# Two groups of weight tiles by seven products, and prelu by a minimum on GpSimd, in blocks 3 to 5 of a retention and feed-forward kernel

## The chip, the cores and the metric

The kernel runs on one core of a Trainium2 chip. The metric is the device time of one execution in microseconds. An execution uses five engines: TensorE (PE in the profile, PEld for its weight loads), VectorE (DVE), ScalarE (ACT), GpSimd (POOL) and SyncE (SP), which only issues transfers. Each engine runs its own list of instructions in order, and semaphores make one wait for another.

## The reference

The first part is a linear attention with a decaying state; the second is a feed-forward layer with a prelu that has one alpha for each of its 2048 hidden columns.

```python
for t in range(S):                                   # 768 steps, 4 batches, 8 heads, 64 wide
    state = gamma * state + k[:, :, t] (x) v[:, :, t]
    y[:, :, t] = scale * q[:, :, t] @ state
x = y.transpose(0, 2, 1, 3).reshape(B * S, H * D)    # 3072 tokens by 512
h = x @ w_in                                         # 512 by 2048
g = np.maximum(h, 0.0) + alpha * np.minimum(h, 0.0)
out = g @ w_out                                      # 2048 by 512
```

## The kernel before

**Blocks.** The 3072 tokens are cut into six blocks (n = 0 to 5) of 512. The attention is done in chunks of 128 tokens, four a block; its result for block n + 1 is made while the feed-forward of block n runs, and lands transposed in `xT`, in two halves of 256 tokens. The order of all instructions is written out by hand: Python generators (`ffn1_mix`, `seven`) yield after each matmul, and `tick(gen, m)` draws m matmuls from one, so the order of the calls in the source is the order on every engine.

**First product, one tile.** A tile of the 2048 hidden columns has 128 of them, so there are sixteen. A whole tile is four matmuls of 512 tokens into one PSUM bank (`full`, L919), then a relu of the negative on ScalarE (L906) and `oma * relu(-h) + h` on VectorE, with oma = 1 - alpha (L910). That is the prelu.

**First product, seven products.** From block 3 on, tiles 0, 1, 8 and 9 are done by a Winograd-Strassen scheme: seven products of sums of halves of x and of w_in replace eight. One product is four matmuls of 256 columns (`part`, L934). The sums of w_in (`win_sum`, four of them) are made once, on GpSimd in block 2; the four sums of x (`x_sum`) for each block, two on VectorE and two on GpSimd. Three PSUM banks are used: products 1, 6, 7 and 4 add up in one (b), product 2 has one (a), products 5 and 3 add up in one (c). After products 1, 6 and 7 ScalarE copies bank b to SBUF (`kept`, L966), and the next product that adds to b must wait for that copy. Then VectorE adds another bank to a copy (L970): for product 2, for product 7 (it reads bank c, so product 3 must wait for it), and for product 3. The three results C get their prelu in `ends`: a relu on ScalarE, then on GpSimd a product with oma (L983) and a sum (L989). The fourth result, in bank b after product 4, is done on ScalarE and VectorE like a whole tile. `MIX` (L897) is the order: 1 to 7 are the products, 0 is a whole tile.

**Second product.** `seven` (L783) multiplies the prelu's result G (`gt`) with w_out by the same scheme, each product being 16 matmuls of 256 columns (L790). It needs sums of G (`g_sums`, L763, with the operation itself in L738): which 0 and 1 make `gs`, 2 makes `third`, 3 subtracts into `gt`; part 0 and 1 are the two halves of the tiles, None is both. The order on PE is: two products of plain G (L790 `ops<-wout,gt`), one of `gs` 1, one of `gs` 0, one of `third`, and two more of G; output sums (`os`, L820) lie between.

**Around it.** In blocks 2 to 4, PE does the scores and states of the next block's chunks between the first and the second product. The k and q of a chunk are scaled to f16 first (`scaled`: one GpSimd operation, L137, or eight on ScalarE, L129), and `turn` transposes them by DMA. In `ffn1_mix`, after eight matmuls, the last chunk (u0 + 3) is scaled, k and q both on GpSimd. `decay` and `sums` carry the state on VectorE (L203, L215) and GpSimd (L217).

Of the kernel before, what the change touches and what calls it, by code (L numbers as in the profile page):

```python
# [9 lines left out]
FP = mybir.dt.float32  # L10
# [5 lines left out]
SUB = mybir.AluOpType.subtract  # L16


@with_exitstack
def kernel(  # L20
# [10 lines left out]
    nc = tc.nc  # L31
# [49 lines left out]
    oma_sb, seen, warm = small[:, 0:NFT], small[:, 32:48], small[:, 64:65]  # L81
    w_in_all = sbp.tile([128, 4, d_ff], F16, tag="win", name="win")
# [785 lines left out]
    wins, xsum = [], []  # L868

    def win_sum(i, eng):  # L870
        if not wins:
            wins.append(sbp.tile([128, 4, 2, 256], F16, tag="gs2", bufs=1, name="wins"))
        t = wins[0]
        a = [[w_in_all[:, 2 * l : 2 * l + 2, 1024 * j : 1024 * j + 256] for l in range(2)] for j in range(2)]
# [22 lines left out]
    MIX = [1, 2, 0, 5, 6, 0, 7, 0, 0, 4, 3] + 8 * [0]  # L897

    def ffn1_mix(n):
        fts = [f for i in range(2, HF) for f in (i, i + HF)]  # L900
        x = xT[n]
        h, bk, later = {}, {}, []
# [31 lines left out]
        def part(s, i):  # L934
# [4 lines left out]
            b, w, t = bk[at], wins[0], xsum[0]  # L939
            for ff in range(2):  # L940
                f = slice(128 * ff, 128 * ff + 128)
                f8 = slice(1024 + 128 * ff, 1152 + 128 * ff)
                for kk in range(2):
                    lhsT, rhs = (
                        (w_in_all[:, kk, f], x[:, 0, kk, :]),
                        (w_in_all[:, 2 + kk, f], x[:, 0, 2 + kk, :]),
                        (w[:, 3, kk, f], x[:, 1, 2 + kk, :]),
                        (w_in_all[:, 2 + kk, f8], t[:, 3, kk, :]),
                        (w[:, 0, kk, f], t[:, 0, kk, :]),
                        (w[:, 1, kk, f], t[:, 1, kk, :]),  # L950
                        (w[:, 2, kk, f], t[:, 2, kk, :]),
                    )[i - 1]
                    nc.tensor.matmul(  # L953
                        out=b[:, 256 * ff : 256 * ff + 256],
                        lhsT=lhsT,
                        rhs=rhs,
                        start=first and ff == 0 and kk == 0,
                        stop=kk == 1,
                        skip_group_check=True,
                    )  # L960
                    yield
# [5 lines left out]
            if i in (2, 7, 3):  # L967

                to = h[{2: 1, 7: 7, 3: 6}[i]]
                nc.vector.tensor_tensor(out=to, in0=bk["a" if i == 2 else "c"], in1=to, op=ADD)  # L970
                later.append((s, to, {2: (0, 0), 7: (HF, 256), 3: (0, 256)}[i]))
            if i == 4:
                hm = relu(b, "hm")
                for ff in range(2):
                    at = slice(256 * ff, 256 * ff + 256)
                    prelu(HF + ff, slice(0, 256), hm[:, at], b[:, at])

        def ends():
            while later:
                _, to, (f, t) = later.pop(0)  # L980
                hm = relu(to, "uv")
                hv, v = [a.rearrange("p (f t) -> p f t", f=2) for a in (hm, to)]
# [6 lines left out]
                nc.gpsimd.tensor_tensor(  # L989
                    out=gt_at(n, slice(f, f + 2), slice(t, t + 256)), in0=hv, in1=v, op=ADD  # L990
                )

        for s, step in enumerate(MIX):
            yield from part(s, step) if step else full()
            if later and s - later[0][0] >= (2 if later[0][0] > 1 else 3):
                ends()
# [207 lines left out]
    ucast(3, 1, A)  # L1204
    w_sums(1, G, [0])
# [45 lines left out]
    for n in range(1, NBLK):  # L1251
        more = n + 1 < NBLK
        u0 = UB * (n + 1)
        if n == 2:
# [14 lines left out]
            for i in range(4):  # L1269
                win_sum(i, G)  # L1270
            for _ in gen:
                pass
        elif n > 2:
# [3 lines left out]
            if more:  # L1277

                scaled(u0 + 3, "k", G)
# [22 lines left out]
        if more:  # L1302
# [118 lines left out]
```

## Time and profile before

| what | us |
|---|---|
| median of 3 runs | 200.2 |
| the three runs | 198.96, 200.2, 201.06 |
| span of the profiled execution | 196.5 |

The page names no time of the profiled execution other than its span. A row of a timeline has the start and duration in us, the engine, the line of the kernel, the operation, output and inputs, and the shape; `x8` means eight of them run on, with the duration from the first start to the last end; in brackets stands the idle time before it. A row of the groups by line has the busy time, then the mean of one in ns. An operation's duration holds the time that it waits for its operands once it has been issued. PE rows overlap by the pipeline: what a stretch costs is the distance from its start to the next row's start. `hm` is a relu's result, `kept` a copy of a bank, `os` an output tile, `hps` and `ops` are PSUM banks.

### The profile page before, as it was taken

To read this page: it belongs to the slowest core of one execution; us is meant where nothing else is said; L and a number is where in the kernel's file an instruction comes from. 1 tells how busy PE (TensorE), PEld (TensorE's weight loads), DVE (VectorE), ACT (ScalarE), POOL (GpSimd) and SP (SyncE) were. 2 spreads that over 40 slices of the span, in tenths; PEclk is the share of its full clock that TensorE was granted. 3 is DMA by queue.
4 is the path that set the end of the run, shared out by engine and by line. 5 is a ranking of instruction groups with operands and counts; after the bars stand their busy time and mean duration, and the time that the engine had idled before them with its cause. 6 is when DMAs were issued, how large, how long until landed. Compare 5 with 4: busy or idle time off the path is not lost.

```text
span 196.5 us, 6453 instructions
## 1 busy us (share of the span) xinstructions
PE 188.7 (96%) x2668; PEld 131.3 (67%) x2668; DVE 151.4 (77%) x258; ACT 119.1 (61%) x265; POOL 149.0 (76%) x151
## 2 busy tenths in 40 slices
PE   7879999999999989999999999999999999999993
PEld 5657544558668878644788754888654888655882
DVE  2697987164989897588978879967789977798922
ACT  3377763238676954477549987749987334686210
POOL 3368989999999576999379999499999296678000
PEclk9999999999999999999999999999999999999999
DMA  6999999999898999999998999992860013100014
GB/s 170 326 361 400 408 384 284 328 360 195 180 244 132 184 306 225 212 282 240 226 222 201 213 224 224 244 215 83 184 189 2 3 57 110 57 0 0 0 58 160
DMA packets 92749, 38.78 MB, mean 197 GB/s; under 512 B 70176, under 2 KB 88624, under 8 KB 92720
## 3 DMA queue, kind: packets, MB, share of 16 engines
q1 hardware_dynamic: 91440, 37.36, 75.8%
q10 hardware_dynamic: 1280, 1.01, 1.6%
q8 instruction: 21, 0.34, 0.7%
q14 instruction: 8, 0.07, 0.1%
HBM read 27.35 MB, written 6.29 MB: 171 GB/s over the span
## 4 chain that ended last, share of the span: by engine, by line
PE 75%; DVE 5%; POOL 5%; DMA 4%; ACT 3%; issue 2%; SPq 2%; POOLq 1%; DVEq 0%; ACTq 0%
PE ops L790 25%; PE hps L620 12%; PE hps L923 11%; PE hps L648 9%; PE ops L715 5%; PE hps L953 3%; DMA qu<-in_q_dram 2%; SPq L340 2%; POOL gt L989 2%; ACT kq L129 2%; PE ops L684 2%; DMA kt<-kq 2%; POOL hm L983 2%; PE ya L522 1%; POOLq L1416 1%
## 5 line engine op out<-in xcount | busy, mean ns | idle before, releaser
L790 PEld LDWEIGHTS <-gt 128*128 128x128 f16 x320 | 30.6, 98 | 4.1
L923 PE MATMUL hps<-xT,win 128*128 128x512 f16 x144 | 33.0, 379 | 0.0
L910 DVE SCALAR_TENSOR_TENSOR gt<-hm,small,hps 128x512 f16<-128x512 f32 (+1 forms) x42 | 28.7, 706 | 5.1 <-ACT hm L906 3.8
L790 PE MATMUL ops<-wout,gt 128*128 128x256 f16 x240 | 28.4, 273 | 0.0
L906 ACT ACTIVATE hm<-hps 128x512 f32<-128x512 f32 x39 | 23.1, 593 | 6.1 <-PE hps L923 5.4
L620 PE MATMUL hps<-xT,win 128*128 128x512 f16 x112 | 24.5, 379 | 0.0
L630 DVE SCALAR_TENSOR_TENSOR gt<-hm,small,hps 128x512 f16<-128x512 f32 x28 | 20.9, 747 | 3.8 <-ACT hm L629 0.9
L923 PEld LDWEIGHTS <-win 128*128 128x128 f16 x144 | 14.1, 98 | 14.4
L137 POOL TENSOR_TENSOR kq<-kqs,tab 128x512 f16<-128x512 f32 x23 | 23.6, 1050 | 0.0
L629 ACT ACTIVATE hm<-hps 128x512 f32<-128x512 f32 x28 | 16.7, 597 | 9.3 <-PE hps L620 9.3
L662 DVE SCALAR_TENSOR_TENSOR gt<-hm,small,hps 128x256 f16<-128x256 f32 x40 | 17.1, 477 | 4.3 <-ACT hm L657 4.3
L808 ACT ACTIVATE kept<-ops 128x512 f32<-128x512 f32 x15 | 9.0, 597 | 18.4 <-PE ops L790 18.4
L620 PEld LDWEIGHTS <-win 128*128 128x128 f16 x112 | 11.0, 98 | 12.8
L217 POOL TENSOR_TENSOR t<-ss,tab 128x256 f16<-128x256 f32 x13 | 8.7, 670 | 14.0 <-DVE ss L215 14.0
L790 PE MATMUL ops<-wsum,gs 128*128 128x256 f16 x160 | 19.1, 273 | 0.2 <-DVE os L820 0.2
L738 POOL TENSOR_TENSOR gt<-gt,gs 128x1024 f16<-128x1024 f16 x8 | 17.0, 2125 | 2.3 <-PE ops L790 2.3
L648 PE MATMUL hps<-xT,win 128*128 128x256 f16 x160 | 18.3, 273 | 0.0
L129 ACT ACTIVATE kq<-kqs,tab 128x64 f16<-128x64 f32 x72 | 18.1, 337 | 0.0
L648 PEld LDWEIGHTS <-win 128*128 128x128 f16 x160 | 15.4, 98 | 2.4
L790 PEld LDWEIGHTS <-gs 128*128 128x128 f16 x160 | 15.1, 98 | 2.4 <-issue 0.4
L820 DVE TENSOR_TENSOR os<-ops,kept 128x512 f32<-128x512 f32 (+1 forms) x17 | 10.5, 624 | 6.5 <-ACT kept L808 4.6
L657 ACT ACTIVATE hm<-hps 128x512 f32<-128x512 f32 x20 | 11.8, 597 | 5.5 <-PE hps L648 3.9
(132 smaller groups left out, 388.5 us busy)
## 6 DMA issues: line engine op xcount, KB each, us to landing
out_dram<-os SPq DMA_DIRECT2D x20, 256.0 KB, 3.5
wi<-in_moe_w_in_dram SPq DMA_DIRECT2D x8, 512.0 KB, 7.7
wo<-in_moe_w_out_dram SPq DMA_DIRECT2D x8, 512.0 KB, 8.5
kqs<-in_k_dram SPq DMA_DIRECT2D x16, 256.0 KB, 4.3
kqs<-in_q_dram SPq DMA_DIRECT2D x16, 256.0 KB, 4.2
vs<-in_v_dram SPq DMA_DIRECT2D x16, 256.0 KB, 4.9
ku<-in_k_dram SPq DMA_DIRECT2D x4, 256.0 KB, 4.1
qu<-in_q_dram SPq DMA_DIRECT2D x4, 256.0 KB, 4.7
```

Source lines behind the costliest of these rows:

```text
L129: eng.activation(out=kqs[u][:, a, h % 4, h // 4, :], in_=staged[u][nm][:, h, :], func=COPY, bias=0.0, scale=tab[:, H * a + h : H * a + h + 1],
L137: eng.tensor_tensor(out=kqs[u][:, a].rearrange("p i r d -> p r i d"), in0=staged[u][nm].rearrange("p (r i) d -> p r i d", i=4), in1=tab[:, ...
L620: nc.tensor.matmul(out=hps, lhsT=w_in_all[:, hp, 128 * ft : 128 * ft + 128], rhs=xT[n][:, :, hp, :], start=(hp == 0), stop=(hp == 3),)
L629: nc.scalar.activation(out=hm, in_=hps, func=RELU, bias=0.0, scale=-1.0)
L630: nc.vector.scalar_tensor_tensor(out=gt_at(n, ft, slice(0, TB)), in0=hm, scalar=oma_sb[:, ft : ft + 1], in1=hps, op0=MULT, op1=ADD,)
L648: nc.tensor.matmul(out=hps[:, 256 * (ft - f0) : 256 * (ft - f0) + 256], lhsT=w_in_all[:, hp, 128 * ft : 128 * ft + 128], rhs=xT[n][:, half ...
L662: nc.vector.scalar_tensor_tensor(out=gt_at(n, f, to), in0=hm[:, at], scalar=oma_sb[:, f : f + 1], in1=hps[:, at], op0=MULT, op1=ADD,)
L738: eng.tensor_tensor(out=out, in0=a, in1=b, op=op)
L790: nc.tensor.matmul(out=bk[:, 256 * t : 256 * t + 256], lhsT=a[:, f, 128 * t : 128 * t + 128], rhs=w[:, f, :], start=first and f == 0 and ( ...
L906: nc.scalar.activation(out=t, in_=src, func=RELU, bias=0.0, scale=-1.0)
L910: nc.vector.scalar_tensor_tensor(out=gt_at(n, f, cols), in0=hm, scalar=oma_sb[:, f : f + 1], in1=src, op0=MULT, op1=ADD,)
L923: nc.tensor.matmul(out=hps, lhsT=w_in_all[:, hp, 128 * ft : 128 * ft + 128], rhs=x[:, :, hp, :], start=(hp == 0), stop=(hp == 3),)
```

## The change

In `ffn1_mix` a second group, tiles 2, 3, 10 and 11, is done by seven products as well, so eight whole tiles are left of twelve. `MIX` gets one list for each group; one whole tile, not two, stands between products 7 and 4. The relu and the GpSimd product of the ends are replaced by two GpSimd operations, (alpha - 1) * min(C, 0), one for each tile of 256 columns, and the sum after them stays. The ends are issued right behind their VectorE sum, no longer two or three steps later. `noma_sb` = alpha - 1 is made once on GpSimd.

Work is moved with it. All four sums of x go to VectorE. The four sums of w_in of the second group are made on VectorE in block 2. The scaling of k of chunk u0 + 3 goes from GpSimd to ScalarE. In blocks 3 to 5 the sums of G are four on VectorE (part 1, then part 0), and `third` part 0 is on GpSimd behind the ends; in block 5 part 1 of `third` is there too.

```diff
-    MIX = [1, 2, 0, 5, 6, 0, 7, 0, 0, 4, 3] + 8 * [0]
+    MIX = [1, 2, 0, 5, 6, 0, 7, 0, 4, 3], [1, 0, 2, 5, 6, 0, 7, 0, 4, 3]
...
-                hm = relu(to, "uv")
...
-                nc.gpsimd.tensor_tensor(
-                    out=hv,
-                    in0=hv,
-                    in1=oma_sb[:, f : f + 2].unsqueeze(2).to_broadcast([128, 2, 256]),
-                    op=MULT,
...
+        def end(to, f, t):
+            hm = sbp.tile([128, 512], FP, tag="uv", bufs=2, name="hm")
+            for ff in range(2):
+                at = slice(256 * ff, 256 * ff + 256)
+                nc.gpsimd.tensor_scalar(
+                    out=hm[:, at],
+                    in0=to[:, at],
+                    scalar1=0.0,
+                    scalar2=noma_sb[:, f + ff : f + ff + 1],
+                    op0=MIN,
+                    op1=MULT,
                 )
...
-            if s == 15:
-                g_sums(n, 0, 2 if n + 1 < NBLK else 0, nc.gpsimd)
-            if s == 17 and n + 1 == NBLK:
-                g_sums(n, 0, 1, nc.vector)
...
-                scaled(u0 + 3, "k", G)
+                scaled(u0 + 3, "k", A)
...
-            ((0, 1), (1, 0), (1, 1)) if n == 1 else ((None, 0), (None, 1)) if more else ((1, 0), (1, 1))
+            ((0, 1), (1, 0), (1, 1))
+            if n == 1
+            else ((None, 0), (None, 1))
+            if n == 2
+            else ((1, 0), (1, 1), (0, 0), (0, 1))
         ):
             g_sums(n, p, w, V)
+        if n > 2:
+            g_sums(n, 0, 2, G)
         if not more:
-            g_sums(n, 0, 2, V)
-            g_sums(n, 1, 2, V)
+            g_sums(n, 1, 2, G)
...
+                if n == 2:
+                    win_sum(1, 0, V)
+                    win_sum(1, 1, V)
                 tick(gen, 15)
                 decay(pb[1])
+                if n == 2:
+                    win_sum(1, 2, V)
+                    win_sum(1, 3, V)
...
-                x_sum(n + 1, 2, G)
-                x_sum(n + 1, 3, G)
+                x_sum(n + 1, 2)
+                x_sum(n + 1, 3)
```

ScalarE at the start of block 3 before, from the last xT copy on; `kq` is the scaled k and q, `kept<-hps` the copy of product 1, then of product 6:

```order
L600 ACTIVATE xT_2348<-yb 128x4x64
L129 ACTIVATE kq_2379<-kqs_2004,tab 128x64 x8
L966 ACTIVATE kept<-hps 128x512
L906 ACTIVATE hm<-hps 128x512
L966 ACTIVATE kept<-hps 128x512
L906 ACTIVATE hm<-kept 128x512
L906 ACTIVATE hm<-hps 128x512
L966 ACTIVATE kept<-hps 128x512
```

The same place now:

```order
L602 ACTIVATE xT_2349<-yb 128x4x64
L131 ACTIVATE kq_2380<-kqs_2005,tab 128x64 x8
L979 ACTIVATE kept<-hps 128x512
L131 ACTIVATE kq_2562<-kqs_2010,tab 128x64 x8
L918 ACTIVATE hm<-hps 128x512
L979 ACTIVATE kept<-hps 128x512
L918 ACTIVATE hm<-hps 128x512
L979 ACTIVATE kept<-hps 128x512
```

Eight more scalings stand between the first copy and the first relu, and the relu of `kept` is gone.

VectorE at the end of block 2 before; the first `os` frees the bank of PE's last product, `xT` is the input of block 3:

```order
L203 TENSOR_TENSOR t_15_2365<-t_15_2355,sta 128x256
L820 TENSOR_TENSOR os<-ops,kept 128x512
L215 TENSOR_TENSOR ss_2401<-t_15_2365,stb 128x256
L820 TENSOR_TENSOR os<-kept,ops 128x512
L599 TENSOR_TENSOR xT_2348<-ya,zs 128x4x64
```

And now:

```order
L205 TENSOR_TENSOR t_15_2366<-t_15_2356,sta 128x256
L740 TENSOR_TENSOR wins_2382<-win 128x512
L740 TENSOR_TENSOR wins_2382<-wins_2382,win 128x512
L822 TENSOR_TENSOR os<-ops,kept 128x512
L217 TENSOR_TENSOR ss_2405<-t_15_2366,stb 128x256
L740 TENSOR_TENSOR wins_2382<-win 128x512
L740 TENSOR_TENSOR wins_2382<-win,wins_2382 128x512
L822 TENSOR_TENSOR os<-kept,ops 128x512
L601 TENSOR_TENSOR xT_2349<-ya,zs 128x4x64
```

Two sums of w_in stand ahead of each output sum, and all four ahead of xT.

GpSimd in block 5 before, to the end of the program:

```order
L983 TENSOR_TENSOR hm<-hm,small 128x512
L989 TENSOR_TENSOR gt_3856<-hm,kept 128x2x256
L983 TENSOR_TENSOR hm<-hm,small 128x512
L989 TENSOR_TENSOR gt_3856<-hm,kept 128x2x256
L983 TENSOR_TENSOR hm<-hm,small 128x512
L989 TENSOR_TENSOR gt_3856<-hm,kept 128x2x256
L738 TENSOR_TENSOR gs_3965<-gt_3856 128x1024
```

The last three of six ends, and what follows them, now:

```order
L996 TENSOR_SCALAR hm<-kept,small 128x256 x2
L1004 TENSOR_TENSOR gt_3924<-hm,kept 128x2x256
L996 TENSOR_SCALAR hm<-kept,small 128x256 x2
L1004 TENSOR_TENSOR gt_3924<-hm,kept 128x2x256
L996 TENSOR_SCALAR hm<-kept,small 128x256 x2
L1004 TENSOR_TENSOR gt_3924<-hm,kept 128x2x256
L740 TENSOR_TENSOR third<-gt_3924 128x1024 x2
```

Three more ends stand ahead of these, and two halves of `third` come behind them in place of a half of `gs`.

More of the change, by code (lines that the diff above doesn't have):

```diff
@@ L81 @@
     oma_sb, seen, warm = small[:, 0:NFT], small[:, 32:48], small[:, 64:65]
+    noma_sb = small[:, 80:96]
     w_in_all = sbp.tile([128, 4, d_ff], F16, tag="win", name="win")
@@ L863, in seven, with win_sum @@
             late_stores.append(put(0, 1, c, u2))
[L868 to L874, printed above, removed]
+    wins, xsum = {}, []
+    def win_sum(g, i, eng):
+        if g not in wins:
+            tag = ("gs2", "wi1")[g]
+            wins[g] = sbp.tile([128, 4, 2, 256], F16, tag=tag, bufs=1, name=f"wins{g}")
+        t = wins[g]
+        a = [
+            [
+                w_in_all[:, 2 * l : 2 * l + 2, 1024 * j + 256 * g : 1024 * j + 256 * g + 256]
+                for l in range(2)
+            ]
+            for j in range(2)
+        ]
         x, y, op = (
@@ L894, in x_sum @@
         minus(eng, t[:, i], x, y)
-    MIX = [1, 2, 0, 5, 6, 0, 7, 0, 0, 4, 3] + 8 * [0]
+    MIX = [1, 2, 0, 5, 6, 0, 7, 0, 4, 3], [1, 0, 2, 5, 6, 0, 7, 0, 4, 3]
     def ffn1_mix(n):
-        fts = [f for i in range(2, HF) for f in (i, i + HF)]
+        mix = [i and (g, i) for g, m in enumerate(MIX) for i in m]
+        groups = len(MIX)
+        fts = [f for i in range(2 * groups, HF) for f in (i, i + HF)]
+        mix += [0] * (len(fts) - mix.count(0))
         x = xT[n]
-        h, bk, later = {}, {}, []
+        h, bk = {}, {}
         def relu(src, tag):
@@ L1204 @@
     ucast(3, 1, A)
+    nc.gpsimd.tensor_scalar(
+        out=noma_sb, in0=oma_sb, scalar1=-1.0, scalar2=0.0, op0=MULT, op1=ADD
+    )
     w_sums(1, G, [0])
```

44 lines of the change are left out of this document (22 added, 22 removed).

## The prediction

> **What bounds the kernel.** I read the page's busy table first, then the timeline of each engine in blocks 2 to 5, then the groups by line for prices.
>
> ```profile
> span 196.5 us, 6453 instructions
> PE 188.7 (96%) x2668; PEld 131.3 (67%) x2668; DVE 151.4 (77%) x258; ACT 119.1 (61%) x265; POOL 149.0 (76%) x151
> ```
>
> PE is busy 96% of the span, so a wait of PE of any length is paid almost in full, and a matmul saved is gained in full. The other engines have room on average only; what matters is which of them ends last where PE needs it. PE in block 5, from product 7 of the seven on (start, duration, then the instruction):
>
> ```profile
> 170.89 1.89 PE L923 MATMUL hps<-xT,win 128*128 128x512 f16 x8
> 172.61 0.60 PE L953 MATMUL hps<-xsum,win 128*128 128x256 f16 x4
> 173.05 0.60 PE L953 MATMUL hps<-xT,wins 128*128 128x256 f16 x4
> 173.49 7.07 PE L923 MATMUL hps<-xT,win 128*128 128x512 f16 x32
> 180.39 3.67 PE L790 MATMUL ops<-wout,gt 128*128 128x256 f16 x32
> 183.91 1.91 PE L790 MATMUL ops<-wsum,gs 128*128 128x256 f16 x16
> ```
>
> From start to next start: 32 matmuls of 512 columns take 6.90 us, 0.216 each, a whole tile (four) 0.86; four of 256 columns take 0.44, 0.11 each.
>
> **The saving.** A second group replaces 16 x 0.216 = 3.45 us by 28 x 0.11 = 3.08: 0.37 us a block, 1.1 us over three blocks.
>
> **Product 3 waits (all three blocks).** Product 3 writes into the bank that the sum for product 7 reads, and that sum needs the copy of product 7. ScalarE and VectorE there, in block 5:
>
> ```profile
> 170.28 0.62 ACT L906 ACTIVATE hm<-kept 128x512 f32<-128x512 f32 x1
> 170.80 0.59 ACT L906 ACTIVATE hm<-hps 128x512 f32<-128x512 f32 x1
> 171.28 0.60 ACT L966 ACTIVATE kept<-hps 128x512 f32<-128x512 f32 x1
> ...
> 171.42 0.75 DVE L910 SCALAR_TENSOR_TENSOR gt<-hm,small,hps 128x512 f16<-128x512 f32 x1 [1.12 <-ACT hm L906]
> 172.09 0.68 DVE L970 TENSOR_TENSOR kept<-hps,kept 128x512 f32<-128x512 f32 x1
> ```
>
> Before, product 7 ended at 170.89, the sum at 172.77, and product 3 came at 173.05 behind two whole tiles and product 4: no wait. Now one whole tile stands there, so PE is at product 3 0.86 us sooner, at 172.2. The relu of C (170.28) is gone from ScalarE, so the copy ends near 171.7, but the sum still stands behind the prelu of the tile before (ends near 171.95) and ends near 172.6. PE waits 0.45 us, in each of the two groups: 0.9, against 0.37 saved. Block 5's first product then takes 0.55 us longer to its end, at 181.0.
>
> **Product 7 waits (blocks 3 and 4).** Eight scalings of k stand newly on ScalarE between the copy of product 1 and the first relu. Block 3 before:
>
> ```profile
> 109.33 2.01 ACT L129 ACTIVATE kq<-kqs,tab 128x64 f16<-128x64 f32 x8
> 111.23 0.58 ACT L966 ACTIVATE kept<-hps 128x512 f32<-128x512 f32 x1
> 111.71 0.58 ACT L906 ACTIVATE hm<-hps 128x512 f32<-128x512 f32 x1
> 112.50 0.60 ACT L966 ACTIVATE kept<-hps 128x512 f32<-128x512 f32 x1 [0.20 <-PE hps L953]
> ...
> 113.16 0.60 PE L953 MATMUL hps<-xsum,wins 128*128 128x256 f16 x4
> ...
> 123.84 3.67 PE L790 MATMUL ops<-wout,gt 128*128 128x256 f16 x32
> 127.34 3.22 PE L790 MATMUL ops<-wsum,gs 128*128 128x256 f16 x28
> ```
>
> The new eight run 111.73 to 113.63 (1.90 to the next start, as 109.33 to 111.23), the relu 0.49, the copy of product 6 114.1 to 114.7. Product 7 adds to the bank that is copied: it starts at 114.75 and not at 113.16, 1.6 us late. Behind it come product 3's waits, 0.3 and 0.5 (in the first group VectorE is freer), less the 0.37: the stage ends 2.0 us later, so 123.84 becomes 125.8. Taking this off GpSimd saves it 1.05 us, which hides nothing here, since GpSimd then waits for that late sum. The data of k is loaded long before; the transpose behind it on SP, and the loads behind that, serve the next block.
>
> **GpSimd's chain.** An end of C was a relu on ScalarE and two GpSimd operations; now it is two TENSOR_SCALAR of 128x256 and the add. No row shows that operation. Rows near it, and what follows on VectorE:
>
> ```profile
> L1070 POOL CAST win<-wi 128x256 f16<-128x256 f32 x5 | 2.0, 436 | 0.0
> L989 POOL TENSOR_TENSOR gt<-hm,kept 128x512 f16<-128x512 f32 x9 | 11.5, 1273 | 0.7
> ...
> 0.80 0.36 POOL L1075 MEMSET mi<- 128x320 f16 x1 [0.29 <-POOLq L1405]
> ...
> 128.21 0.61 POOL L217 TENSOR_TENSOR t<-ss,tab 128x256 f16<-128x256 f32 x1 [3.37 <-DVE ss L215]
> ...
> 122.70 2.13 POOL L738 TENSOR_TENSOR third<-gt 128x1024 f16<-128x1024 f16 x1
> ...
> 181.97 0.74 DVE L910 SCALAR_TENSOR_TENSOR gt<-hm,small,hps 128x512 f16<-128x512 f32 x1
> 182.74 0.69 DVE L738 TENSOR_TENSOR gs<-gt 128x1024 f16<-128x1024 f16 x1
> ```
>
> I take 0.41 from the CAST (one source, same size; 2.0 us for five); the ends are the memset's 0.36 and the two-source 0.61. An end costs 2 x 0.41 + 1.27 = 2.09 us. The Trainium skill, GPSIMD Engine Reference, section Elementwise, gives a one-source loop 1.03 cycles an element, an estimate of 0.22 us here; by it the sum below would be 17.5 and not 18.9. In block 5 the sum for product 7 is there at 172.6, and five ends follow almost without a gap: 172.65 + 5 x 2.09 = 183.1. In block 3 it is there at 116.8 and they end at 127.5 (127.25, and a gap of 0.25 ahead of the sum for product 3). Block 4 has the same order and is taken like block 3. Only then can the last two of VectorE's four sums of G run, and the first product of G sums (183.91 and 127.34 above) waits for the last of them.
>
> **The four sums against GpSimd.** They read two SBUF tensors, as the sums of x do:
>
> ```profile
> 135.59 3.04 POOL L137 TENSOR_TENSOR kq<-kqs,tab 128x512 f16<-128x512 f32 x3
> ...
> 137.79 1.13 DVE L738 TENSOR_TENSOR xsum<-xT 128x512 f16<-128x512 f16 x1
> ...
> 166.44 0.43 DVE L738 TENSOR_TENSOR xsum<-xT 128x512 f16<-128x512 f16 x1
> ```
>
> Alone the sum takes 0.43; beside GpSimd it takes 1.13 and ends at 138.92, 0.29 after GpSimd's operation (135.59 + 3.04). So such a sum waits out the GpSimd operation it meets, and each sum that waits for the one before lets one GpSimd operation in. Block 5: the last prelu ends at 182.6, sum 1 waits for the end's add and is done at 183.7, third 0 runs to 185.7 (2.13), sum 2 to 186.2, third 1 to 188.15, sum 3 to 188.7, sum 4 to 189.4. PE starts at 189.45 and not at 183.91: 5.5 us, with the 0.55 in it. Blocks 3 and 4: sum 1 ends at 128.0, third 0 at 130.0 (the other third comes later there), then 130.5, 131.1, 131.85; PE starts at 131.9 and not at 127.34: 4.6 us each, the 2.0 in it. Behind the four sums on VectorE stand the state sums, an output sum and the masks of the next pair; PE asks for the masks 28 matmuls after that start (3.22 us), and both move alike, so nothing is added; third 1 and the two subtractions behind it on GpSimd move with the state sums by the same 4.6.
>
> Two pages of the Trainium skill differ here. Perfetto Trace Analysis, section Optimizing Scalar/DVE Operations, gives the lock to a 2-port VectorE operation, which a TENSOR_TENSOR is not: by it the sums would not wait, and the time would be the second rival's, 207.1. SBUF — State Buffer, section Who interferes with whom, adds operations with two SBUF inputs, and with it the time is 219.1; the trace's 1.13 against 0.43 is on that side.
>
> **Four sums of w_in on VectorE in block 2.** The same waiting:
>
> ```profile
> 105.27 2.13 POOL L738 TENSOR_TENSOR gt<-gt,gs 128x1024 f16<-128x1024 f16 x1
> 107.35 3.23 POOL L137 TENSOR_TENSOR kq<-kqs,tab 128x512 f16<-128x512 f32 x3
> ...
> 105.35 0.42 DVE L203 TENSOR_TENSOR t<-t,sta 128x256 f16<-128x256 f16 x1 [0.18 <-POOL t L217]
> 106.09 0.69 DVE L820 TENSOR_TENSOR os<-ops,kept 128x512 f32<-128x512 f32 x1 [0.31 <-ACT kept L808]
> ...
> 108.26 0.42 DVE L599 TENSOR_TENSOR xT<-ya,zs 128x256 f16<-128x256 f32 x1 [0.36 <-ACT zs L591]
> ...
> 107.00 0.38 PE L790 MATMUL ops<-wout,gt 128*128 128x256 f16 x2
> ```
>
> Sum 1 stands behind the row at 105.35, waits until 107.4 and ends at 107.7; one scaling goes in (1.08), sum 2 ends at 108.9. The output sum of 106.09 comes at 108.9, and PE's last product, which writes into the bank it reads, at 109.6 and not 107.00: 2.6 us. Sums 3 and 4 meet the other two scalings and end near 111.6; the xT rows come near 112.0 and not 108.26, the ScalarE row of 109.33 behind them 4.2 us late, and product 6 of block 3 waits for the copy behind that. I take 4.2; the ends are 2.6, if ScalarE's lateness hides, and 4.5.
>
> **No cost taken.** Two more sums of x on VectorE: products 7 and 4, which need them, wait for copies anyway. The last block's two thirds on GpSimd are in the chain above. One 128x16 operation on GpSimd early on lies beside its casts.
>
> **The sum.** 4.2 + 4.6 + 4.6 + 5.5 = 18.9 us, the saving of 1.1 in it. The page gives the profiled execution no time but its span, 196.5; the median of the runs is 200.2, so 3.7 us lie around the span, kept as they are. 196.5 + 18.9 + 3.7 = 219.1.
>
> **Rivals.** First, VectorE keeps its turn at each meeting and its sums run in a row. For it: the trace has few meetings. Against: the scaling after the first sum of x did go in between. Block 2 about 2, blocks 3 and 4 127.5 plus four sums, 130.05, so 2.7 each, block 5 185.8, so 1.9: 9.3 us, 209.5.
>
> Second, the sums do not wait at all. Against: the 1.13. Block 2 0.8 (two sums in VectorE's queue), blocks 3 and 4 four sums of 0.69 from the last prelu, 129.6, 2.3 each; block 5 185.4, 1.5: 6.9 us, 207.1.
>
> Third, not slower: ScalarE's copies are not what PE waits for, because the k scalings start before the copy of product 1 is due and end ahead of it, and GpSimd's chain then starts early enough to be done when PE is. It decides if product 7 of block 3 starts within 0.2 us of its turn. Against: the order has them behind that copy. PE then only saves: 1.1 us less, 199.1.
>
> **The numbers.** Forecast 0.62, first rival 0.18, second 0.08, third 0.08, more gain than the matmuls give 0.04. About 1% of the time is what a measurement of this kernel can tell from no change. So faster by over 1% 0.04, within 1% 0.08 (the third rival), slower 0.88. At 0.61 us an operation the chain adds 1.3 us in each of blocks 3 and 4, 221.7 with the rest as it is; a little more for block 2 makes 223. Downwards the range takes in both slower rivals and ends at 206: 206 to 223 holds a little over 0.8.
>
> **What would show it.** Right: product 7 of blocks 3 and 4 behind a copy that follows eight scalings; product 3 about 0.4 us behind a VectorE sum in every group; sums of G of 1 to 2.5 us beside GpSimd; a PE wait of 2 to 5 us ahead of the first product of G sums, longest in block 5. Wrong: sums of G near 0.69 beside a busy GpSimd (first or second rival), a TENSOR_SCALAR far from 0.41, or PE without these gaps.

## The result, and the profile after

The changed kernel takes 243.7 us (median of 4 runs, 241.6 to 245.6) against 199.6 (198.9 to 201.1) for the kernel before: a ratio of 1.215, 95% interval 1.207 to 1.224. The profiled execution took 243.84, its span is 242.1. The forecast was 219.1 with a range of 206 to 223: slower was right, the size was not.

The page of the changed kernel: the span, PE's busy row, the granted clock in 40 slices, the chain that ended last by engine and by line, and the two groups of GpSimd operations that an end of C now consists of (busy us, mean ns of one, then idle before them).

```profile
span 242.1 us, 6574 instructions
...
PE 196.9 (81%) x2704; PEld 137.8 (57%) x2704; DVE 165.9 (69%) x274; ACT 117.8 (49%) x272; POOL 189.2 (78%) x181
...
PEclk9999999999999999999999968999995699998579
...
POOL 31%; PE 8%; DVE 5%; issue 5%; ACT 1%; POOLq 0%; DVEq 0%
POOL hm L996 16%; POOL gt L1004 9%; PE ops L792 7%; DVE gs L740 4%; POOL gt L740 3%; POOL kq L139 1%; POOL t L219 1%; POOL third L740 1%; ACT kept L979 0%; ACT hm L918 0%; DVE ss L217 0%; DVE t L205 0%; DVE kept L983 0%; DVE os L822 0%; PE ya L295 0%
...
L996 POOL TENSOR_SCALAR hm<-kept,small 128x256 f32<-128x256 f32 x36 | 42.0, 1176 | 11.1 <-DVE kept L983 11.1
...
L1004 POOL TENSOR_TENSOR gt<-hm,kept 128x512 f16<-128x512 f32 x18 | 23.3, 1293 | 1.5
```

The granted clock and the chain by engine before:

```profile
PEclk9999999999999999999999999999999999999999
...
PE 75%; DVE 5%; POOL 5%; DMA 4%; ACT 3%; issue 2%; SPq 2%; POOLq 1%; DVEq 0%; ACTq 0%
```

PE was busy 96% of the span before, now 81%. The chain that ended last was PE's before (75% of the span); now the half of the span over which it is followed back is GpSimd's for the most part (31%), 25% on the two lines of the ends. One TENSOR_SCALAR takes 1176 ns, where the forecast had 410. The row of PE's granted clock (9 is 90% or more), which had no dip before, now has one in each of blocks 3 to 5.

GpSimd in block 3 (start, duration, instruction): the first of the six ends, the last, and the difference of G behind it.

```profile
118.02 2.28 POOL L996 TENSOR_SCALAR hm<-kept,small 128x256 f32<-128x256 f32 x2 [3.42 <-DVE kept L983]
120.38 1.27 POOL L1004 TENSOR_TENSOR gt<-hm,kept 128x512 f16<-128x512 f32 x1
...
137.02 2.26 POOL L996 TENSOR_SCALAR hm<-kept,small 128x256 f32<-128x256 f32 x2
139.36 1.26 POOL L1004 TENSOR_TENSOR gt<-hm,kept 128x512 f16<-128x512 f32 x1
140.70 2.62 POOL L740 TENSOR_TENSOR third<-gt 128x1024 f16<-128x1024 f16 x1
```

From 118.02 to 140.6 is 22.6 us for six ends, about 3.6 each and a gap of 0.6. VectorE's four sums of G stand around the last of them:

```profile
132.08 1.49 DVE L740 TENSOR_TENSOR gs<-gt 128x1024 f16<-128x1024 f16 x1
133.60 0.85 DVE L740 TENSOR_TENSOR gs<-gs,gt 128x1024 f16<-128x1024 f16 x1
140.66 0.69 DVE L740 TENSOR_TENSOR gs<-gt 128x1024 f16<-128x1024 f16 x1 [6.21 <-POOL gt L1004]
141.38 2.49 DVE L740 TENSOR_TENSOR gs<-gs,gt 128x1024 f16<-128x1024 f16 x1
```

The third sum waits 6.21 us for the last end; the fourth takes 2.49 because it waits out GpSimd's difference (140.70 + 2.62 = 143.32). PE in block 3 from product 6 of the first group on, and in block 5 (the bracket is the idle time ahead of the row, and what ended it):

```profile
117.24 0.60 PE L966 MATMUL hps<-xsum,wins 128*128 128x256 f16 x4 [1.03 <-ACT kept L979]
117.68 1.03 PE L935 MATMUL hps<-xT,win 128*128 128x512 f16 x4
120.11 0.60 PE L966 MATMUL hps<-xsum,wins 128*128 128x256 f16 x4 [1.41 <-ACT kept L979]
...
127.42 0.60 PE L966 MATMUL hps<-xsum,win 128*128 128x256 f16 x4
128.31 0.60 PE L966 MATMUL hps<-xT,wins 128*128 128x256 f16 x4 [0.29 <-DVE kept L983]
...
133.07 3.45 PE L792 MATMUL ops<-wout,gt 128*128 128x256 f16 x30 [1.48 <-POOL gt L1004]
143.93 4.96 PE L792 MATMUL ops<-wsum,gs 128*128 128x256 f16 x28 [7.40 <-DVE gs L740]
...
216.81 3.45 PE L792 MATMUL ops<-wout,gt 128*128 128x256 f16 x30 [2.50 <-POOL gt L1004]
227.65 6.18 PE L792 MATMUL ops<-wsum,gs 128*128 128x256 f16 x32 [7.39 <-DVE gs L740]
```

PE waits 7.4 us for the sums of G. And the 28 matmuls behind that wait take 4.96 us; before the change the same 28 took 3.22. Two stretches of the trace (from:to, length, busy us and count of PE, PEld, DVE, ACT, POOL, then PE's granted clock) say why:

```profile
143.90:147.40 3.50, 3.47 (x17) 2.48 (x18) 2.84 (x6) 0.00 (x0) 2.60 (x2) 0.50 0.21 75
147.40:150.00 2.60, 2.60 (x141) 2.23 (x139) 0.00 (x0) 0.84 (x3) 2.18 (x2) 0.98 0.00 0
```

For the first 3.5 us behind the wait the clock is granted at 0.50. In block 2, VectorE's new sums of w_in push an output sum back, and PE's last product waits for its bank:

```profile
107.51 1.99 DVE L740 TENSOR_TENSOR wins<-win 128x512 f16<-128x512 f16 x1
109.53 1.15 DVE L740 TENSOR_TENSOR wins<-wins,win 128x512 f16<-128x512 f16 x1
110.61 0.68 DVE L822 TENSOR_TENSOR os<-ops,kept 128x512 f32<-128x512 f32 x1
```

```profile
111.34 0.38 PE L792 MATMUL ops<-wout,gt 128*128 128x256 f16 x2 [2.16 <-DVE os L822]
```

Stage by stage, from the starts on PE in both traces, the 45.6 us of the span lie here:

| stretch | before | after | longer by |
|---|---|---|---|
| start to block 2's first output product | 95.09 | 96.91 | 1.8 |
| from there to block 3's first product | 14.46 | 16.97 | 2.5 |
| from there to block 3's first product of G sums | 17.79 | 30.05 | 12.3 |
| from there to block 4's first product | 10.84 | 12.58 | 1.7 |
| from there to block 4's first product of G sums | 17.88 | 29.88 | 12.0 |
| from there to block 5's first product | 10.86 | 13.54 | 2.7 |
| from there to block 5's first product of G sums | 16.99 | 27.72 | 10.7 |
| from there to the end | 12.59 | 14.45 | 1.9 |

The first row is not the change's: in the experiments below that product starts between 94.3 and 97.4, without order. So the experiments are also compared by the time from there to the end of the span, 101.4 us before and 145.2 after.

### The profile page after: what moved, and what is told of

It reads as the page before. It is cut to its first block, busy times and chain, and to the rows that moved or that the text cites. A ratio compares the mean times of both kernels' runs of the same rounds, so it can differ in the third digit from the quotient of the medians.

```text
span 242.1 us, 6574 instructions
## 1 busy us (share of the span) xinstructions
PE 196.9 (81%) x2704; PEld 137.8 (57%) x2704; DVE 165.9 (69%) x274; ACT 117.8 (49%) x272; POOL 189.2 (78%) x181
## 4 chain that ended last, share of the span: by engine, by line
POOL 31%; PE 8%; DVE 5%; issue 5%; ACT 1%; POOLq 0%; DVEq 0%
POOL hm L996 16%; POOL gt L1004 9%; PE ops L792 7%; DVE gs L740 4%; POOL gt L740 3%; POOL kq L139 1%; POOL t L219 1%; POOL third L740 1%; ACT kept L979 0%; ACT hm L918 0%; DVE ss L217 0%; DVE t L205 0%; DVE kept L983 0%; DVE os L822 0%; PE ya L295 0%
## 5 line engine op out<-in xcount | busy, mean ns | idle before, releaser
L996 POOL TENSOR_SCALAR hm<-kept,small 128x256 f32<-128x256 f32 x36 | 42.0, 1176 | 11.1 <-DVE kept L983 11.1
L792 PE MATMUL ops<-wsum,gs 128*128 128x256 f16 x160 | 25.9, 334 | 22.2 <-DVE gs L740 22.2
L922 DVE SCALAR_TENSOR_TENSOR gt<-hm,small,hps 128x512 f16<-128x512 f32 (+1 forms) x36 | 22.6, 656 | 8.6 <-ACT hm L918 7.7
L622 PE MATMUL hps<-xT,win 128*128 128x512 f16 x112 | 24.7, 379 | 0.1
L1004 POOL TENSOR_TENSOR gt<-hm,kept 128x512 f16<-128x512 f32 x18 | 23.3, 1293 | 1.5
L935 PE MATMUL hps<-xT,win 128*128 128x512 f16 x96 | 24.1, 379 | 0.0
L131 ACT ACTIVATE kq<-kqs,tab 128x64 f16<-128x64 f32 x88 | 22.1, 336 | 0.0
L631 ACT ACTIVATE hm<-hps 128x512 f32<-128x512 f32 x28 | 16.7, 597 | 9.6 <-PE hps L622 9.6
L740 DVE TENSOR_TENSOR gs<-gt 128x1024 f16<-128x1024 f16 (+1 forms) x8 | 7.9, 990 | 19.6 <-POOL gt L1004 19.5
L918 ACT ACTIVATE hm<-hps 128x512 f32<-128x512 f32 x30 | 17.2, 594 | 7.8 <-PE hps L935 7.0
L740 POOL TENSOR_TENSOR third<-gt 128x1024 f16<-128x1024 f16 x8 | 18.9, 2365 | 0.2
L622 PEld LDWEIGHTS <-win 128*128 128x128 f16 x112 | 10.9, 98 | 13.2 <-POOL win L1066 0.7
```

The costliest lines, as they stand in the source:

```text
L131: eng.activation(out=kqs[u][:, a, h % 4, h // 4, :], in_=staged[u][nm][:, h, :], func=COPY, bias=0.0, scale=tab[:, H * a + h : H * a + h + 1],
L622: nc.tensor.matmul(out=hps, lhsT=w_in_all[:, hp, 128 * ft : 128 * ft + 128], rhs=xT[n][:, :, hp, :], start=(hp == 0), stop=(hp == 3),)
L740: eng.tensor_tensor(out=out, in0=a, in1=b, op=op)
L792: nc.tensor.matmul(out=bk[:, 256 * t : 256 * t + 256], lhsT=a[:, f, 128 * t : 128 * t + 128], rhs=w[:, f, :], start=first and f == 0 and ( ...
L922: nc.vector.scalar_tensor_tensor(out=gt_at(n, f, cols), in0=hm, scalar=oma_sb[:, f : f + 1], in1=src, op0=MULT, op1=ADD,)
L935: nc.tensor.matmul(out=hps, lhsT=w_in_all[:, hp, 128 * ft : 128 * ft + 128], rhs=x[:, :, hp, :], start=(hp == 0), stop=(hp == 3),)
```

## The experiments

The theory (A) was that the price of the TENSOR_SCALAR carries most of the loss, by the chain of ends and by the clock that falls in the wait; the main rival (B), that the placement does: the sums on VectorE against GpSimd, ScalarE's scalings, block 2. Measured, with the ratio to the kernel before as it was run beside each:

| kernel | us | ratio (95%) | from block 2's output product to the end |
|---|---|---|---|
| e2, old ends | 229.0 | 1.150 (1.141 to 1.159) | 131.2 |
| e3, one group, new ends | 210.5 | 1.057 (1.050 to 1.064) | 112.3 |
| e4, ends of one addition | 217.1 (213.9 to 220.3) | 1.091 (1.081 to 1.102) | |
| e5, wait filled | 236.9 | 1.193 (1.185 to 1.202) | 139.0 |
| e6, k on GpSimd | 243.4 | 1.223 (1.214 to 1.232) | 145.8 |
| e7, w_in sums on GpSimd | 242.6 | 1.218 (1.209 to 1.226) | 143.9 |
| e8, third on VectorE | 237.8 | 1.195 (1.188 to 1.201) | 138.7 |
| e9, cheap ends | 207.6 | 1.042 (1.037 to 1.047) | 110.0 |
| e10, e9 with the new ends | 228.2 | 1.143 (1.135 to 1.150) | 130.6 |
| e11, e9 with one group | 199.9 | 1.000 (0.996 to 1.004) | 101.3 |
| e12, e9 in another order | 207.0 | 1.040 (1.036 to 1.045) | 109.2 |

**What the operation costs alone (e1).**

```diff
+    for _ in range(3):
+        G.tensor_scalar(out=py[:, H0], in0=px[:, H0], scalar1=0.0, scalar2=al, op0=MIN, op1=MULT)
+    for _ in range(3):
+        G.tensor_scalar(out=py[:, H0], in0=px[:, H0], scalar1=0.0, scalar2=-0.75, op0=MIN, op1=MULT)
+    for _ in range(3):
+        G.tensor_scalar(out=py[:, H0], in0=px[:, H0], scalar1=-1.0, scalar2=0.5, op0=MULT, op1=ADD)
...
```

> The kernel before with rows of operations on GpSimd appended behind its last work, three of each form, so that each form is seen alone; they write to scratch tiles and leave the output as it is. Theory A (the operation is expensive by itself): the TENSOR_SCALAR of 128x256 with min and a multiplication by a column takes 1.1 to 1.2 us with the other engines idle, and 128x512 in one instruction twice that. Rival B (it is cheap by itself and was slowed by what ran beside it on the other engines in the changed kernel): 0.36 to 0.61 us alone, as the prediction had it. What makes it dear is open: if the column operand does, the form with two immediates falls back to about 0.4; if min does, the form with multiplication and addition falls back; if the two operations in one instruction do, the forms with one operation fall back. The 128x256 CAST stays at 0.40 and the 128x256 sum of two sources at 0.61.

The groups on GpSimd. L1408 is the change's form (min with 0, multiplication by a column), L1410 the same with an immediate factor, L1412 multiplication and addition of immediates, L1414 min alone, L1416 multiplication by a column alone, L1406 a copy:

```profile
L1408 POOL TENSOR_SCALAR py<-px,small 128x256 f32<-128x256 f32 x3 | 3.4, 1142 | 0.3
L1410 POOL TENSOR_SCALAR py<-px 128x256 f32<-128x256 f32 x3 | 3.2, 1066 | 0.3
L1416 POOL TENSOR_SCALAR py<-px,small 128x256 f32<-128x256 f32 x3 | 2.8, 923 | 0.3
L1414 POOL TENSOR_SCALAR py<-px 128x256 f32<-128x256 f32 x3 | 2.5, 848 | 0.2
L1412 POOL TENSOR_SCALAR py<-px 128x256 f32<-128x256 f32 x3 | 1.2, 407 | 0.2
L1406 POOL COPY py<-px 128x256 f32<-128x256 f32 x3 | 1.2, 401 | 0.2
```

And the change's form on VectorE:

```profile
L1422 DVE TENSOR_SCALAR py<-px,small 128x256 f32<-128x256 f32 x3 | 1.3, 425 | 29.8 <-POOL py L1418 29.7
```

A holds: 1.14 us with the other engines idle, so nothing beside it made it dear. None of the three guesses at the reason is right by itself: two operations in one instruction are as cheap as a copy (407 ns) if they are a multiplication and an addition of immediates, but min alone takes 848 and a column alone 923. On VectorE the change's form takes 425. The sum of two sources took 0.72 us, where 0.61 was expected.

**The ends as before the change (e2).**

```diff
-            hm = sbp.tile([128, 512], FP, tag="uv", bufs=2, name="hm")
-            for ff in range(2):
...
-                nc.gpsimd.tensor_scalar(
...
+            hm = relu(to, "uv")
+            nc.gpsimd.tensor_tensor(
+                out=hm.rearrange("p (f t) -> p f t", f=2),
+                in0=hm.rearrange("p (f t) -> p f t", f=2),
+                in1=oma_sb[:, f : f + 2].unsqueeze(2).to_broadcast([128, 2, 256]),
+                op=MULT,
+            )
```

> The changed kernel with the ends of C as before the change (relu on ScalarE two or three steps later, on GpSimd a multiplication and an addition of 128x512, 1.04 and 1.27 us); two groups and everything else stay as changed. Theory A (GpSimd's chain of six ends, made long by the TENSOR_SCALAR, is what PE waits for, and the granted clock falls in that wait): six ends take 14.1 us and not 21.5, PE's wait ahead of the first product of G sums falls from 7.4 us to under 2 us, the product behind it goes back from 4.96 to about 3.3 us, and the time is 212 to 220 us. Rival B (the sums of G waiting out GpSimd, the sums of w_in in block 2 and ScalarE's k scalings carry most of the loss, whatever an end costs): over 232 us.

229.0: between the two. The ends alone took some 14 of the 44 us away. VectorE's sums of G in block 3 show what stayed:

```profile
133.44 2.60 DVE L740 TENSOR_TENSOR gs<-gt 128x1024 f16<-128x1024 f16 x1
136.08 0.69 DVE L740 TENSOR_TENSOR gs<-gs,gt 128x1024 f16<-128x1024 f16 x1
```

The last of six ends is done at 132.97 (they start only at 118.09, behind the relu on ScalarE), the third sum still meets GpSimd's difference, PE waits 3.7 us, and of the product behind it the first 18 matmuls take 3.49 us. A's number was too low because it let the other terms vanish with the chain.

**One group, new ends (e3).**

```diff
-                hm = relu(to, "uv")
-                nc.gpsimd.tensor_tensor(
...
+                for ff in range(2):
+                    at = slice(256 * ff, 256 * ff + 256)
+                    nc.gpsimd.tensor_scalar(
...
```

> The kernel before with its one group of seven products, its order and its placement of all other work, and only the new ends of C (two TENSOR_SCALAR and the addition on GpSimd, no relu). Theory A: three ends take 10.8 us and not 7.1; in block 3 they end near 126.3 in the times of the kernel before, 1.5 us after VectorE could start the sums of G, so blocks 3 and 4 lose 1.1 to 1.5 us each and block 5 about 1: 202 to 204.5 us. Rival B (an end is cheap, 2.1 us): the ends end sooner than before and the time is that of the kernel before, 199 to 200.5 us.

210.5, so B's "cheap" is out, and A's number is too low by 6. The ends are done at 126.74 as worked out (126.3), but then GpSimd's difference and VectorE's second sum meet:

```profile
126.82 3.16 POOL L740 TENSOR_TENSOR third<-gt 128x1024 f16<-128x1024 f16 x1
```

```profile
128.03 3.02 DVE L740 TENSOR_TENSOR gs<-gs,gt 128x2048 f16<-128x2048 f16 x1
```

```profile
131.11 4.90 PE L792 MATMUL ops<-wsum,gs 128*128 128x256 f16 x28 [3.13 <-DVE gs L740]
```

The sum that took 1.23 us before takes 3.02, PE waits 3.13, and its 28 matmuls take 4.90, not 3.22. One late chain is paid three times.

**Ends of one addition (e4).**

```diff
-            hm = sbp.tile([128, 512], FP, tag="uv", bufs=2, name="hm")
-            for ff in range(2):
...
+            hm = to
```

> The changed kernel with the two TENSOR_SCALAR of each end left out (the addition adds C to itself, so the negative slope of prelu is missing for these tiles); groups, order and placement as changed. Theory A: an end is 1.27 us, GpSimd is never the last, and what stays is block 2's VectorE sums (2.5 us), products 6, 7 and 3 waiting for ScalarE and VectorE (3.0, 1.9 and 0.5 us in blocks 3, 4, 5) and up to 2 us for the four sums of G: 206 to 211 us, with the granted clock back above 0.98. Rival B (placement and exclusion carry most of the loss): over 225 us.

217.1 lies between the two. Leaving the two operations out takes some 27 of the 44 us away, but some 17 stay, more than A had. Its trace is read for what waits, not for its length (the profiled execution took 218.8): PE still waits 1.5, 1.8 and 4.0 us for the sums of G, of which the first takes 2.17 beside GpSimd's difference, and behind the last wait 32 matmuls take 6.38 us.

**The wait filled (e5).**

```diff
+        if n > 2:
+            z = bank(k + 2, "wps")
+            for _ in range(30):
+                nc.tensor.matmul(out=z, lhsT=wz[:, 0:128], rhs=wz, start=True, stop=True)
         store = put(0, 0, a, s1)
```

> The changed kernel, and in blocks 3 to 5 thirty matmuls of 512 columns on zeros (30 x 0.216 = 6.5 us at the full clock) put into a free bank between the second product of the sequence and the first product of G sums, where PE waits 7.4 us anyway. They compute nothing that is used. Theory A (the idle wait itself lowers the granted clock, so the product behind it runs at half rate at first): the 28 matmuls behind the wait go back from 4.96 and 5.8 to about 3.3 us, the 32 of block 5 from 6.0 to about 3.9, and the time falls by 5 to 6.5 us, to 237 to 239 us. Rival (that product is slow for another reason, its operands for example): no gain, 242 to 246 us, as the wait is only filled.

236.9, just under A's 237 to 239. PE in block 3, behind thirty matmuls that nobody needs:

```profile
142.57 3.23 PE L792 MATMUL ops<-wsum,gs 128*128 128x256 f16 x28 [0.95 <-DVE gs L740]
```

The wait still ends with VectorE's last sum, but the product behind it runs in 3.23 us, as before the change (3.22). So the idle wait itself lowers the clock, at 6 us in three blocks.

**k on GpSimd, sums of w_in on GpSimd (e6, e7).**

```diff
-                scaled(u0 + 3, "k", A)
+                scaled(u0 + 3, "k", G)
```

> The changed kernel with the scaling of k in blocks 3 and 4 back on GpSimd. Theory A (GpSimd's chain of ends sets the end of the stage): product 7 of the first group no longer waits 1.4 us, but the first end starts when it did, the second 0.6 us sooner, and PE waits for the chain the longer: 0.5 to 1.5 us less in all, 242 to 243 us. Rival (the eight scalings on ScalarE are what costs): 1.5 to 2 us less in each of the two blocks, 239.5 to 240.5 us.

243.4, a little above A's range and no difference that can be measured. By the trace product 7 comes on time in both blocks, and yet 145.8 us lie behind block 2's output product, against 145.2: the wait of product 7 is hidden as long as GpSimd's chain ends last. In block 3 a wait for an end lowered the clock here (0.67 granted in the first 3.2 us behind it):

```profile
132.29 5.12 PE L792 MATMUL ops<-wout,gt 128*128 128x256 f16 x30 [2.37 <-POOL gt L1004]
```

```diff
-            for i in range(4):
-                win_sum(0, i, G)
+            for g in range(2):
+                for i in range(4):
+                    win_sum(g, i, G)
...
-                    win_sum(1, 0, V)
-                    win_sum(1, 1, V)
```

> The changed kernel with the four sums of w_in for the second group on GpSimd, behind those for the first group in block 2, where GpSimd idles 4.2 us. Their price on VectorE was forecast at 4.2 us; by the profile of the changed kernel it is about 2.5 (an output sum 2.2 us late and PE with it). Theory A: 2 to 3 us less, 240.5 to 241.7 us, PE's wait ahead of block 2's last product gone. By the forecast 4.2 us less, 239.5. Rival (they were never in the way): 243 to 245 us.

242.6, between the two: the ratio can't be told from the changed kernel's; by the trace it gains 1.3 us (143.9 against 145.2). PE's wait fell to 0.55 us, but on GpSimd the sums met VectorE's sums of G, and here GpSimd waited too:

```profile
98.51 2.01 POOL L740 TENSOR_TENSOR wins<-wins,win 128x512 f16<-128x512 f16 x1
100.49 2.13 POOL L740 TENSOR_TENSOR wins<-win 128x512 f16<-128x512 f16 x1
102.58 1.16 POOL L740 TENSOR_TENSOR wins<-win,wins 128x512 f16<-128x512 f16 x1
```

**The third difference on VectorE (e8).**

```diff
         if n > 2:
-            g_sums(n, 0, 2, G)
+            g_sums(n, 0, 2, V)
         if not more:
-            g_sums(n, 1, 2, G)
+            g_sums(n, 1, 2, V)
```

> The changed kernel with the difference of G for the third factor (128x1024) on VectorE behind its four sums in blocks 3 to 5, not on GpSimd beside them. Theory A (a VectorE sum of two SBUF tensors waits out the GpSimd operation it meets): the third of the four sums takes 0.69 us and not 2.5, so each block gains about 1.8 us; VectorE's additional 0.69 us lies behind what PE waits for: 237 to 240 us. Rival (the sums do not exclude each other; the long ones are long for another reason): 243 to 245 us.

237.8, as A had it. VectorE in block 3:

```profile
139.92 0.69 DVE L740 TENSOR_TENSOR gs<-gt 128x1024 f16<-128x1024 f16 x1 [6.22 <-POOL gt L1004]
140.65 0.69 DVE L740 TENSOR_TENSOR gs<-gs,gt 128x1024 f16<-128x1024 f16 x1
```

With nothing on GpSimd beside it the last sum takes 0.69 us and not 2.49.

**Two groups placed otherwise, with cheap and with dear ends (e9, e10, e11).** Built from the kernel before. The relu on ScalarE takes the column as its scale, so GpSimd only adds:

```diff
+    MIX2 = [1, 2, 0, 5, 6, 0, 7, 0, 4, 11, 3, 12, 0, 15, 16, 0, 17, 0, 14, 0, 13, 0]
...
+        two = n in (3, 4)
...
-                hm = relu(to, "uv")
+                for ff in range(2):
+                    at = slice(256 * ff, 256 * ff + 256)
+                    nc.scalar.activation(out=hm[:, at], in_=to[:, at], func=RELU, bias=0.0,
+                        scale=noma_sb[:, f + ff : f + ff + 1])
```

> Built from the kernel before: two groups in blocks 3 and 4 (block 5 keeps one), and an end of C made of a relu on ScalarE that already multiplies by the column (1 - alpha), two of 128x256, and one addition of 128x512 on GpSimd (1.27 us). The second group's sums of w_in run on VectorE early, before block 1; k stays on GpSimd, behind the first ends; the third difference of blocks 3 and 4 is on VectorE behind the masks. Theory A (two groups cost nothing where GpSimd's six ends are done when VectorE's sums of G start: 6 x 1.27 = 7.6 us against 7.1 before): PE gains 2 x 0.37 us less a few tenths in waits, 197.5 to 200 us, within 1% of the kernel before. Rival (two groups cost by themselves, through the waits of products and the sums of G): 202 to 207 us.

> The kernel of the first run of this call with one difference: the relu on ScalarE is replaced by the two TENSOR_SCALAR on GpSimd, as in the change, in all three blocks. Theory A (the size of that operation on GpSimd is what costs): an end is 3.6 us, six take 21.5 us, blocks 3 and 4 lose about 12 us each to the chain and 2 each to the clock behind the wait, block 5 about 1: 224 to 233 us. Rival (with the rest of the change placed well, the chain hides): under 212 us.

> The kernel of the first run of this call with one group in blocks 3 and 4 as well; the second group's sums of w_in still run early. The control for what a second group saves. Theory A: PE bound as the kernel before, 198 to 200.5 us; the first run of this call is 0.3 to 0.8 us shorter, if its waits do not eat that.

e10 against e9 is the cleanest price of the operation: one difference (in e9 ScalarE's relu does the multiplication), 228.2 against 207.6 us, 20.6 us (130.6 - 110.0 by the traces too). e11 against the kernel before: the cheaper end and the early sums cost nothing. But e9 against e11 went to the rival, 0.6 above its range: a second group in blocks 3 and 4 costs 8 us and saves nothing. (With it the third difference of these two blocks moves to VectorE, which e11 leaves on GpSimd; the two were not taken apart.) PE's waits in e9, block 3 and the stage behind it; the third is the first product of G sums, and block 4 has the same wait by VectorE's sum:

```profile
PE hps L965 <- ACT kept L978: 1.4, 2, 1.1
PE stb L189 <- DVE kept L982: 0.8, 1, 0.8
PE ops L791 <- ACT kq L130: 0.8, 1, 0.8
PE yb L294 <- DVE t L204: 0.8, 1, 0.8
```

3.8 us a block, against the 0.37 that a group was to save on PE.

**Another order (e12).**

```diff
-    MIX2 = [1, 2, 0, 5, 6, 0, 7, 0, 4, 11, 3, 12, 0, 15, 16, 0, 17, 0, 14, 0, 13, 0]
+    MIX2 = [1, 2, 0, 5, 6, 0, 7, 0, 4, 11, 3, 12, 15, 0, 16, 0, 17, 0, 14, 13, 0, 0]
...
-            while later:
+            if later:
```

> The kernel of the run with cheap ends (two groups in blocks 3 and 4, one addition of GpSimd an end, 207.6 us), where each of these blocks waits 3.8 us in four places: for the copy of product 6, for the last sum of C, for the sums of G and for the state behind them. Now a whole tile stands between products 6 and 7 of the second group instead of ahead of 5, two whole tiles behind its product 3 and not one, and ScalarE takes one end at a step and not two in a row. Theory A (the second group's cost that is left is its order, copies and sums that come behind other work): 1.5 to 3 us of the waits go, 203 to 205.5 us. Rival (a second group takes this time in any order, since seven short products with six passes of ScalarE and VectorE between them replace four whole tiles): 206.5 to 209 us. In neither case does it beat the kernel before.

207.0: the rival again. The wait for the copy of product 6 fell from 1.1 to 0.7 us, the states' wait for the last sum of C went, the one for the sums of G rose to 1.1, and waits of 0.4 for a prelu and 0.2 for a sum of C came in. In these two orders the waits move and hardly shrink. Whether a third order pays was not tried, so no version here beats the kernel before.

## Why the prediction was wrong

**The step that failed is the price of the TENSOR_SCALAR**: "I take 0.41 from the CAST (one source, same size; 2.0 us for five); the ends are the memset's 0.36 and the two-source 0.61." It takes 1.14 alone (e1), and in the kernel an end takes 3.60 us from its start to the next end's (125.81 to 129.41 in block 3), not 2.09; both of my bounds were far too low. The rows were chosen for their shape; none of them had the operation, and no row bounded it from above. Put into the prediction's own working (five ends in a row, then the two sums that are left behind them as measured, 0.69 and 2.49) 3.60 gives 10.7, 10.7 and 10.0 us for blocks 3 to 5 in place of 4.6, 4.6 and 5.5; measured were 12.3, 12.0 and 10.7. The rest, 0.7 to 1.6 us a block, lies ahead of that row of ends: by the trace six run almost without a gap, and not five. The mechanism (GpSimd's chain, then VectorE's sums, then PE) was right; e10 against e9 shows its size.

**A term was missing: the clock.** The prediction moved PE's products and left their durations. Of its 4.6 and 5.5 us, 2.6 and 5.0 were to be PE standing still ahead of the sums (the 2.0 and the 0.55 lie before), and what such a wait does to the clock no row of the trace before shows, since its clock row is flat. It costs 1.7, 2.7 and 1.9 us by the table, 6.3 in all, and e5 shows that the idle time is the cause. The Trainium skill, TensorE: Matmul & The Clock Gate, section Part 1: The HAM clock gate, states that the array falls to half its clock behind an idle window of about 3.4 us and needs a busy window of about as much to come back; the trace agrees, with 0.50 granted for the first 3.5 us behind 7.4 us of waiting. By that window only the wait of block 5 was forecast long enough, so half of 3.4, an estimate of 1.7 us, would have come into the sum once. The other two waits became that long by the price of the ends.

With the two, the working gives 196.5 + 10.7 + 10.7 + 10.0 + 4.2 + 6.3 + 3.7 = 242.1 us; measured were 243.7. That it comes so near is partly luck, and the 6.3 is a measured term. The three blocks took 35.0 us and not 31.4 and 1.8 lie in the first stretch; against that, block 2 took 2.5 and not 4.2, and around the span lie 1.7 us (243.84 against 242.1), not the 3.7 that the prediction took from a median and the span of another execution.

**Sums of G against GpSimd: right.** The last sum took 2.49 beside the difference of G, 0.69 without it (e8), which is worth 4 to 6 us here. The first and second rival are out with it. The Trainium skill, SBUF — State Buffer, section Who interferes with whom, states that a VectorE instruction with two SBUF inputs contends with a GpSimd instruction that reads SBUF, and the trace agrees, with 2.49 against 0.69. In e3 the late chain itself brought such a meeting about.

**Product 7 and product 3: right.** By the starts, product 7 came 1.57 us late in block 3 (117.68 to 120.11, less the 0.86 of a whole tile) and 1.58 in block 4; 1.6 was forecast, and the third rival is out. Product 3 came 0.28 to 0.41 late in the first group of a block and 0.45 in the second (127.42 to 128.31, less 0.44), where 0.3, 0.5 and, in block 5, 0.45 were forecast. The brackets show less (1.41, 0.29), since PE's rows overlap. The first output product came 1.92 us later within block 4 and 0.53 within block 5; 2.0 and 0.55 were forecast. But e6 shows that taking ScalarE's scalings back gains nothing: in a stage that GpSimd ends, the wait of product 7 is only moved into the longer one.

**Block 2: near, and partly hidden.** 4.2 was forecast. Block 3's first product came 2.5 us later behind block 2's first output product (2.2 of it is the wait of PE's last product), and product 6 of block 3 came 1.19 late behind ScalarE's copy, as the prediction had it; with the sums of w_in on GpSimd (e7) that is 0.11. Together 3.7, but the second part lies inside the wait for the chain. Undone the whole is worth about 1 us (e7); there the sums meet VectorE's sums of G.

**Not seen: PE waits for an end before it waits for the sums.** The first output product reads the tiles that product 2 of the second group fills; their end comes 1.5 to 2.5 us late. Behind a longer wait this too costs nothing by itself, except where it lowers the clock.

**The saving of 1.1 us: not there.** Even with cheap ends and another placement the second group makes blocks 3 and 4 about 4 us longer each. That is the largest part that stays without a full account: e9 names the waits (3.8 us a block, in four places) and e12 shows them move, and neither shows a way around them. In the changed kernel e4 puts what is left without the two operations, this part and block 2 with the meetings of sums and the clock behind their waits, at some 17 of the 44 us.

## What to carry to other kernels

A duration is tied to the operation and its operands, not to the shape: where no row has the operation on that engine, its cost has no upper bound from other rows, and the range must say so, or the operation be tried alone first. A late chain is paid more than once: the engine that waits loses the wait, the sums that now meet cost again (1.23 to 3.02 us in e3), and TensorE can come back at half its clock (0.50 behind 7.4 us here). Before replacing long matmuls by short ones, count the passes of the other engines between them; here 28 short matmuls for 16 long ones were to save 0.37 us and brought six more copies and sums for PE to wait for.

## What was not expected of the hardware

- GpSimd, 128x256 in float32: copy 0.40 us, multiplication and addition of immediates 0.41, min alone 0.85, multiplication by a column alone 0.92, min and a factor 1.07, min and a column 1.14; 128x512 of the last 2.00. Min and a column of 128x256 on VectorE took 0.43. The Trainium skill, GPSIMD Engine Reference, section Elementwise, states 1.03 cycles an element, from which the prediction has its estimate of 0.22 us; the measured 1.14 decides here.
- Waiting between VectorE and GpSimd goes both ways: sums of w_in on GpSimd took 2.01 and 2.13 us beside VectorE's sums of G, 1.16 without them (e7).
- A wait much shorter than 7 us can be enough for the half clock, but need not be: thirty matmuls took 5.12 us behind 2.37 in e6 and 3.45 behind 2.50 in the changed kernel, and in e3 28 took 4.90 behind 2.57. These waits are shorter than the window of about 3.4 us named above; the measurement decides.
